# The first weight quarter in two loads of one row each, with three warm-up matmuls fewer

## Chip, cores, metric

The kernel runs on one core of a Trainium2 chip. The metric is device time in microseconds (us). One execution of each kernel was also recorded by the profiler; "the trace" means that one execution. Since it is one of several, its own time is given where that matters.

## The reference, cut

```python
x = A_x                                          # 2048 x 1024, bf16
g = _sigmoid((x * gate_w).sum(-1, keepdims=True))
a = _A_ref(x, A_wqkv, A_wo)                      # linear attention, 32 heads of 32
b = _B_ref(x, B_wqkv, B_wo)                      # sliding dilated attention
return g * a + (1 - g) * b
# in _A_ref:
qkv = x @ wqkv                                   # wqkv: 1024 x 3072, so q | k | v
pq, pk = phi(q), phi(k)
```

The change touches only the very beginning: the k part of A's projection, the first thing that the kernel computes.

## The kernel before: the parts concerned

The weights of k are held in two halves of 512 columns, `WkA[0]` and `WkA[1]`, each with eight "rows" of 128 contraction indices. A "quarter" here is two rows of one half (256 KB). The names used below: the *first* quarter is `WkA[0]` rows 0 and 1, the *second* quarter is `WkA[1]` rows 0 and 1. Two x loads bring 256 of the 1024 columns of token rows 0 to 255 and 256 to 511. TensorE transposes these itself; the rest of x comes transposed by DMA.

```python
def load_wk(eng, k, h):
    eng.dma_start(out=WkA[h][:, 2 * k:2 * k + 2, :],
                  in_=A_wqkv[2 * k * P:(2 * k + 2) * P, D + 512 * h:D + 512 * h + 512]
                  .rearrange("(kt p) n -> p kt n", p=P))
# ... cut
load_wk(nc.scalar, 0, 0)                 # first quarter, on ScalarE's queue
load_rows(nc.sync, 0, 2, 0, 2 * P)       # x rows, on SyncE's queue from here on
load_rows(nc.sync, 2, 4, 0, 2 * P)
load_wk(nc.sync, 0, 1)                   # second quarter
load_xT(1, 0, 4)                         # x transposed by DMA
load_wk(nc.sync, 1, 0)
load_wk(nc.sync, 1, 1)
# ... cut
warm_up(29)                              # 29 matmuls on ones, results unused
# ... cut
transpose_rows(0)
first = [bank_k(i) for i in range(4)]
for kt in range(2):
    for t in range(2):
        project(first[t], t, kt, 0)      # first four real matmuls: first quarter
transpose_rows(2)
first += [bank_k(i) for i in range(4, 8)]
for half, t0 in ((1, 0), (0, 2), (1, 2)):
    for kt in range(2):
        for t in (t0, t0 + 1):
            project(first[4 * half + t], t, kt, half)   # fifth matmul on: second quarter
```

TensorE executes in this order. The last part of the diff concerns `WoB[1]`, weights for the last stage, loaded some 350 us later.

The softmax here doesn't subtract the row's maximum and nothing guards it: scores larger than these inputs give would overflow.

Of the kernel before, what the change touches and what calls it, by code (L numbers as in the profile page):

```python
# [15 lines left out]
P = 128  # L16
# [23 lines left out]
def kernel(  # L40
# [11 lines left out]
    nc = tc.nc  # L52
    S, D = A_x.shape[1:]
# [5 lines left out]
    def rows(ap, s0, s1):  # L59
        return ap[s0 // 1024, s0 % 1024:(s1 - 1) % 1024 + 1, :]  # L60
# [3 lines left out]
    KT = D // P  # L64
# [11 lines left out]
    def load_w(name, src, col0, tag, only=(0, 1)):  # L76
        halves = []
        for h in only:
            w = wpool.tile([P, KT, 512], BF16, name=f"{name}{h}", tag=tag)
            c0 = col0 + h * 512  # L80
            nc.sync.dma_start(out=w[:], in_=src[:, c0:c0 + 512].rearrange("(kt p) n -> p kt n", p=P))
            halves.append(w)
        return halves
# [4 lines left out]
    def load_rows(eng, t0, t1, d0=0, d1=D):  # L88
        eng.dma_start(out=xrow[:, t0:t1, d0:d1],
                      in_=rows(x, t0 * P, t1 * P)[:, d0:d1].rearrange("(t p) d -> p t d", p=P))  # L90

    WkA = [wpool.tile([P, KT, 512], BF16, name=f"WkA{h}", tag="wa") for h in range(2)]

    def load_xT(k, t0, t1):
        nc.sync.dma_start_transpose(out=xT[:, 2 * k:2 * k + 2, t0 * P:t1 * P],
                                    in_=rows(x, t0 * P, t1 * P)[:, 2 * k * P:(2 * k + 2) * P])
# [5 lines that stand above are left out]
# [11 lines left out]
            nc.vector.tensor_tensor(out=ident[q:q + 32, q:q + 32], in0=col[q:q + 32, :], in1=row[q:q + 32, :],  # L113
                                    op=ALU.is_equal)
    with tc.manual_schedule(engines={SP, mybir.EngineType.Activation}):
        load_wk(nc.scalar, 0, 0)
        load_rows(nc.sync, 0, 2, 0, 2 * P)
        load_rows(nc.sync, 2, 4, 0, 2 * P)
        load_wk(nc.sync, 0, 1)
        load_xT(1, 0, 4)  # L120
        load_wk(nc.sync, 1, 0)
        load_wk(nc.sync, 1, 1)
        for k in range(2, 4):
            load_xT(k, 0, 4)
            load_wk(nc.sync, k, 0)
            load_wk(nc.sync, k, 1)
        for t in range(4, NB):
            nc.sync.dma_start_transpose(out=xT[:, :, t * P:(t + 1) * P], in_=rows(x, t * P, (t + 1) * P))
        load_rows(nc.sync, 0, 4, 2 * P, D)
        for t in range(4, NB, 4):  # L130
            load_rows(nc.sync, t, t + 4)
        gw_row = consts.tile([P, D], BF16, name="gw_row")
        nc.sync.dma_start(out=gw_row[:], in_=gate_w.partition_broadcast(P))
        WvA = load_w("WvA", A_wqkv, 2 * D, "wb")
        WoA = load_w("WoA", A_wo, 0, "wo")
        WvB = load_w("WvB", B_wqkv, 2 * D, "wc")
# [49 lines left out]
    with tc.manual_schedule(engines={PE}):  # L186

        with ExitStack() as s1:
# [9 lines left out]
            def warm_up(n):  # L198
                warm = ps_1.tile([P, P], F32, name="warm", tag="p1")
                for i in range(n):  # L200
                    nc.tensor.matmul(warm[:], lhsT=ones, rhs=ones, start=True, stop=True)  # L201


            warm_up(29)
            def transpose_rows(t):
                for kt in range(2):
                    xt = ps_1.tile([P, 2 * P], BF16, name="xt_ps", tag="p1")
                    for i in range(2):
                        nc.tensor.transpose(xt[:, i * P:(i + 1) * P], xrow[:, t + i, kt * P:(kt + 1) * P], ident)  # L209
                    (nc.scalar.copy if kt else nc.vector.tensor_copy)(out=xT[:, kt, t * P:(t + 2) * P], in_=xt[:])  # L210
# [35 lines left out]
            for t in range(1, NB):  # L246
                side.append(lambda t=t: nc.vector.tensor_tensor(
                    out=zacc[:], in0=zacc[:] if t > 1 else pk[:, 0, :], in1=pk[:, t, :], op=ALU.add))
            side.append(lambda: nc.gpsimd.partition_all_reduce(zrow[:], zacc[:], P, bass_isa.ReduceOp.add))
            for t in range(NB):  # L250
                side.append(lambda t=t: nc.vector.tensor_tensor_reduce(
                    out=gjunk[:], in0=xrow[:, t, :], in1=gw_row[:], scale=1.0, scalar=0.0, op0=ALU.mult,
# [139 lines left out]
        with ExitStack() as s2:  # L392
# [157 lines left out]
            WoB = [wpool.tile([P, KT, 512], BF16, name="WoB0", tag="wb")]  # L550

            def load_wo(half, k0, k1):
                for k in range(k0, k1):
                    nc.sync.dma_start(out=WoB[half][:, k, :],
                                      in_=B_wo[k * P:(k + 1) * P, half * 512:(half + 1) * 512])

            for c in range(KT):
                kts[c] = kpool.tile([P, 2, 1024], BF16, name="kt", tag="kt")
                for hh in range(2):
# [3 lines left out]
                    if 1 <= c <= 2:  # L563
                        t = 2 * (c - 1) + hh
                        nc.sync.dma_start_transpose(out=pqT[0][:, :, t * P:(t + 1) * P],
                                                    in_=pqd[t * P:(t + 1) * P, :])
                    if 4 <= c < 7:
# [1 line left out]

            load_wo(0, 6, 8)  # L570
            WoB.append(wpool.tile([P, KT, 512], BF16, name="WoB1", tag="wb"))
            load_wo(1, 0, 4)
            nc.sync.dma_start(out=WoB[1][:, 4:KT, :],
                              in_=B_wo[4 * P:, 512:1024].rearrange("(k p) n -> p k n", p=P))
            raw = wpool.tile([P, 4, D], BF16, name="raw", tag="wc")
            fw = wpool.tile([P, 2, D], F32, name="fw", tag="wc")
            lw = wpool.tile([P, 4, D], BF16, name="lw", tag="wa")
# [112 lines left out]
```

## Time and profile before

| | before |
|---|---|
| median of 3 runs (range) | 472.19 us (471.96 to 472.64) |
| time of the traced run, and its span | 471.98 us, 470.3 us |
| TensorE busy | 466.4 us, 99% |
| first real matmul | 4.75 us |
| fifth, the first to use the second quarter | 5.96 us |
| second quarter landed (semaphore record) | 5.91 us |

"idle before <-releaser" at the end of a timeline line says how long the engine stood and what ended it. Two lines of the timeline of the kernel before belong beside those that the prediction shows, the second transposes and what follows them:

```profile
5.63 0.39 PE L209 MATMUL xt_ps<-pk,xrow 128*128 128x128 bf16 x4
...
5.96 3.41 PE L195 MATMUL pk_ps<-WkA,xT 128*128 128x512 bf16 x15
```

The second line shows no wait, and yet there was one. The instruction records behind these lines have the four transposes start at 5.63, 5.69, 5.74 and 5.80 us, 0.056 us apart, while each is booked 0.22 us long. The last is thus booked until 6.02, and an idle time in front of the fifth matmul can't show, although TensorE was free for it at 5.80 + 0.056 = 5.85 (worked out).

What it waited for is in the trace's semaphore records, which no view prints as such: each load updates its semaphore 16 times, and with the 16th it has *landed*. The second quarter landed at 5.91, and the fifth matmul started 0.05 us later. So TensorE waited about 0.1 us for that load in the kernel before already, and this will matter.

### The profile page before, as it was taken

How to read it: one execution, taken by the hardware profiler on the slowest of the kernel's cores; microseconds unless marked ns; L12 is line 12 of the kernel's file. 1: busy time of each engine (PE TensorE's matmuls, PEld its weight loads, DVE VectorE, ACT ScalarE, POOL GpSimd, SP SyncE). 2: the span in 40 equal slices, each digit the busy share in tenths (PEclk: the TensorE clock that was granted, in tenths of full speed). 3: DMA queues.
4: the chain of work that ended last, by engine and by line, in shares of the span. 5: the costliest groups of instructions: out<-in, count | busy, mean ns of one | idle time of the engine just before them, and what ended most of it. 6: DMA issues, size and time to landing. Idle time of an engine off the chain costs nothing.

```text
span 470.3 us, 13208 instructions
## 1 busy us (share of the span) xinstructions
PE 466.4 (99%) x5765; PEld 266.0 (57%) x5765; DVE 278.1 (59%) x612; ACT 169.6 (36%) x277; POOL 15.3 (3%) x30
## 2 busy tenths in 40 slices
PE   9999999999999999999999999999999999999997
PEld 5444444445444444444888888888764444444444
DVE  2586689990219999999666676667660049800000
ACT  1443321112433333334555555555543134221121
POOL 3300000500000000000000000000000000000000
PEclk9999999999999999999999999999999999999999
DMA  8999960000654243627326525452454933211111
GB/s 242 192 257 366 348 205 0 0 1 1 216 134 123 83 141 123 156 97 252 105 56 106 109 47 97 103 92 55 87 137 102 199 94 79 73 52 45 34 33 46
DMA packets 98188, 55.14 MB, mean 117 GB/s; under 512 B 69074, under 2 KB 90578, under 8 KB 98130
## 3 DMA queue, kind: packets, MB, share of 16 engines
q1 hardware_dynamic: 93106, 49.87, 40.6%
q10 hardware_dynamic: 5024, 4.43, 2.9%
q8 instruction: 45, 0.74, 0.7%
q14 instruction: 13, 0.11, 0.1%
HBM read 26.10 MB, written 15.86 MB: 89 GB/s over the span
## 4 chain that ended last, share of the span: by engine, by line
PE 99%; DVE 0%; issue 0%; DVEq 0%
PE q_ps L419 26%; PE d_ps L625 12%; PE pk_ps L195 12%; PE p_ps L323 12%; PE g_ps L262 12%; PE e_ps L625 12%; PE p_ps L359 9%; PE po L499 2%; PE s2b L477 2%; PE warm L201 1%; PE kv_ps L282 0%; PE w_ps L179 0%; PE xt_ps L209 0%; DVE osb L632 0%; DVE xT L210 0%
## 5 line engine op out<-in xcount | busy, mean ns | idle before, releaser
L419 PE MATMUL q_ps<-xT,WqB 64*64 64x512 bf16 x1024 | 70.1, 376 | 0.0
L419 PE MATMUL q_ps<-xT,WkB 64*64 64x512 bf16 x1024 | 69.7, 376 | 0.0
L170 DVE TENSOR_SCALAR e<-e 128x512 f32<-128x512 f32 x64 | 27.0, 423 | 61.3 <-ACT e L169 61.3
L323 PE MATMUL p_ps<-WvB,xT 128*128 128x512 bf16 x256 | 57.4, 379 | 0.0
L195 PE MATMUL pk_ps<-WkA,xT 128*128 128x512 bf16 x256 | 55.6, 379 | 0.3 <-DVE xT L210 0.3
L262 PE MATMUL g_ps<-pk,xrow 128*128 128x512 bf16 x256 | 55.4, 379 | 0.0
L482 ACT ACTIVATE PT<-s2b 128x928 bf16<-128x928 f32 (+4 forms) x40 | 34.2, 855 | 50.1 <-PE s2b L477 49.1
L484 DVE TENSOR_TENSOR PT<-PT,mask 128x928 bf16<-128x928 bf16 (+4 forms) x40 | 23.6, 589 | 36.3 <-ACT PT L482 36.3
L419 PEld LDWEIGHTS <-WkB 64*64 64x64 bf16 x1024 | 39.7, 107 | 7.3 <-DMA vd<-tmp 0.2
L359 PE MATMUL p_ps<-WqA,xT 128*128 128x512 bf16 x192 | 43.4, 379 | 0.0
L625 PEld LDWEIGHTS <-pqT 128*128 128x128 bf16 x272 | 26.0, 98 | 29.6 <-DMA obd<-Ob 0.2
L625 PEld LDWEIGHTS <-OBT 128*128 128x128 bf16 x272 | 26.0, 98 | 29.4
L262 PEld LDWEIGHTS <-xrow 128*128 128x128 bf16 x256 | 25.0, 98 | 30.2
L419 PEld LDWEIGHTS <-WqB 64*64 64x64 bf16 x1024 | 38.6, 107 | 6.1 <-DVE qz L459 0.2
L195 PEld LDWEIGHTS <-xT 128*128 128x128 bf16 x256 | 24.9, 98 | 30.3 <-DVE xT L210 0.4
L323 PEld LDWEIGHTS <-xT 128*128 128x128 bf16 x256 | 24.9, 98 | 30.2 <-issue 0.5
L632 DVE TENSOR_SCALAR osb<-e_ps,omg 128x128 bf16<-128x128 f32 x1 | 0.3, 350 | 57.6 <-PE e_ps L625 57.6
L328 ACT CAST tmp<-p_ps 128x512 bf16<-128x512 f32 x32 | 18.7, 587 | 38.0 <-PE p_ps L323 33.7
L499 PEld LDWEIGHTS <-PT 64*56 64x56 bf16 (+2 forms) x1152 | 28.9, 104 | 5.5
L169 ACT ACTIVATE e<-pk_ps 128x512 f32<-128x512 f32 x32 | 18.9, 597 | 35.8 <-PE pk_ps L195 31.6
L359 PEld LDWEIGHTS <-xT 128*128 128x128 bf16 x192 | 18.8, 98 | 22.7
L625 PE MATMUL d_ps<-WoA,pqT 128*128 128x512 bf16 (+1 forms) x136 | 30.9, 370 | 0.0
(71 smaller groups left out, 542.1 us busy)
## 6 DMA issues: line engine op xcount, KB each, us to landing
vd<-tmp SPq DMA_DIRECT2D x16, 264.0 KB
out_dram<-osb ACTq DMA_DIRECT2D x31, 128.0 KB
xrow<-in_A_x_dram SPq DMA_DIRECT2D x3, 1024.0 KB
pqd<-tmp SPq DMA_DIRECT2D x12, 256.0 KB
WvA<-in_A_wqkv_dram SPq DMA_DIRECT2D x2, 1024.0 KB
WoA<-in_A_wo_dram SPq DMA_DIRECT2D x2, 1024.0 KB
WvB<-in_B_wqkv_dram SPq DMA_DIRECT2D x2, 1024.0 KB
WqA<-in_A_wqkv_dram SPq DMA_DIRECT2D x2, 1024.0 KB
```

Of the source, the lines that this page charges most:

```text
L169: nc.scalar.activation(out=e[:], in_=pj[:], func=ACT.Exp)
L170: nc.vector.tensor_scalar(out=e[:], in0=e[:], scalar1=1.0, scalar2=1e-6, op0=ALU.min, op1=ALU.add)
L195: nc.tensor.matmul(pj[:], lhsT=xT[:, kt, t * P:(t + 1) * P], rhs=WkA[half][:, kt, :], start=(kt == 0), stop=(kt == KT - 1))
L262: nc.tensor.matmul(pj[:], lhsT=xrow[:, t, kt * P:(kt + 1) * P], rhs=pk[:, t, half * 512:(half + 1) * 512], start=(t == 0), stop=(t == NB - 1))
L323: nc.tensor.matmul(st["pj"][:], lhsT=xT[:, kt, t * P:(t + 1) * P], rhs=WvB[half][:, kt, :], start=(kt == 0), stop=(kt == KT - 1))
L328: nc.scalar.copy(out=v[:, half * 16:(half + 1) * 16, 0:Dh], in_=st["pj"][:].rearrange("p (h e) -> p h e", h=16))
L359: nc.tensor.matmul(st["pj"][:], lhsT=xT[:, kt, t * P:(t + 1) * P], rhs=WqA[half][:, kt, :], start=(kt == 0), stop=(kt == KT - 1))
L419: nc.tensor.matmul(banks[o][64 * j:64 * j + 64, :], lhsT=lhsT(r, kt, j), rhs=rhs(r, kt), start=first and kt == 0, stop=kt == KT - 1, skip_ ...
L482: nc.scalar.activation(out=pt[:, :, 0:W_], in_=s2b[:].rearrange("p a b s -> p (a b) s")[:, :, 0:W_], func=ACT.Exp, scale=SCALE)
L484: nc.vector.tensor_tensor(out=pt[:, :, 0:W_], in0=pt[:, :, 0:W_], in1=mask[:, None, base:base + W_].broadcast_to([P, 4, W_]), op=ALU.mult)
L499: nc.tensor.matmul(o2[64 * h:64 * h + w, par, s_, i, :], lhsT=pt[r, i, o:o + w], rhs=V[r, m, 4 * c + i, :], start=True, stop=True)
L625: nc.tensor.matmul(st["ps"][:, 0:n], lhsT=lhsT, rhs=W[c0 // 512][:, c, c0 % 512:c0 % 512 + n], start=(side == 0 and c == 0), stop=(side == ...
```

## The change

The intent: the x rows, which TensorE waits for first, should not stand behind a whole weight quarter. The quarter is cut in two loads. Three warm-up matmuls are taken out so that TensorE is free when the rows come. The number of loads in all is kept by merging one at the end.

```diff
-        load_wk(nc.scalar, 0, 0)
+        for kt in range(2):
+            nc.scalar.dma_start(out=WkA[0][:, kt, :], in_=A_wqkv[kt * P:(kt + 1) * P, D:D + 512])
...
-            warm_up(29)
+            warm_up(26)
...
-            load_wo(1, 0, 4)
-            nc.sync.dma_start(out=WoB[1][:, 4:KT, :],
-                              in_=B_wo[4 * P:, 512:1024].rearrange("(k p) n -> p k n", p=P))
+            load_wo(1, 0, 3)
+            nc.sync.dma_start(out=WoB[1][:, 3:KT, :],
+                              in_=B_wo[3 * P:, 512:1024].rearrange("(k p) n -> p k n", p=P))
```

## The prediction

> **What bounds the kernel now.** I read the page's busy shares and its chain first, then the waits of TensorE, then the first ten microseconds instruction by instruction, because the change lies almost wholly there.
>
> The page of the kernel before, parts 1 and 4:
>
> ```profile
> span 470.3 us, 13208 instructions
> PE 466.4 (99%) x5765; PEld 266.0 (57%) x5765; DVE 278.1 (59%) x612; ACT 169.6 (36%) x277; POOL 15.3 (3%) x30
> ...
> PE 99%; DVE 0%; issue 0%; DVEq 0%
> ```
>
> TensorE is busy 466.4 of 470.3 us and is 99% of the chain that ended last. So only two things move the time: work taken off TensorE, or idle time ahead of it. Idle time in total is 470.3 - 466.4 = 3.9 us. That is also, within rounding, the most that any change of waits alone can give: 0.8%.
>
> The waits of TensorE's matmuls, then those of its weight loads:
>
> ```profile
> PE warm L201 <- PEq L674: 0.8, 1, 0.8
> PE pk_ps L195 <- DVE xT L210: 0.3, 1, 0.3
> ```
>
> ```profile
> PEld L195 <- DVE xT L210: 0.4, 1, 0.4
> ...
> PEld L209 <- DMA xrow<-in_A_x_dram: 0.2, 1, 0.2
> ```
>
> The columns are total us, number of waits, the longest. The reader is to see two places at the start: the first transposes wait 0.2 us for a transfer of x rows (their weight loads do), and the first real matmul waits 0.3 us for the copy of what was transposed.
>
> The timeline of the start (start, duration, engine, line, operation, count, idle before):
>
> ```profile
> 0.80 0.97 SPq L89 DMA_DIRECT2D xrow<-in_A_x_dram  x2
> 0.81 3.01 PEld L201 LDWEIGHTS <-const-bfloat16-1.0 128*128 128x128 bf16 x29 [0.81 <-issue]
> 0.82 0.47 ACTq L99 DMA_DIRECT2D WkA<-in_A_wqkv_dram  x1
> 0.84 3.25 PE L201 MATMUL warm<-const-bfloat16-1.0 128*128 128x128 bf16 x29 [0.84 <-PEq L674]
> ...
> 3.98 0.33 PEld L209 LDWEIGHTS <-xrow 128*128 128x128 bf16 x4 [0.16 <-DMA xrow<-in_A_x_dram]
> 3.98 0.50 PE L209 MATMUL xt_ps<-pk,xrow 128*128 128x128 bf16 x4
> 4.41 0.29 DVE L210 COPY xT<-xt_ps 128x256 bf16<-128x256 bf16 x1 [0.96 <-PE xt_ps L209]
> 4.52 0.37 ACT L210 COPY xT<-xt_ps 128x256 bf16<-128x256 bf16 x1 [2.44 <-PE xt_ps L209]
> 4.75 0.55 PEld L195 LDWEIGHTS <-xT 128*128 128x128 bf16 x4 [0.44 <-DVE xT L210]
> 4.75 1.04 PE L195 MATMUL pk_ps<-WkA,xT 128*128 128x512 bf16 x4 [0.27 <-DVE xT L210]
> ```
>
> The real work starts at 4.75 us and is unbroken from there. The start time of that matmul is what the change can move. It hangs on transposes (3.98), these on the later of two things: the end of 29 warm-up matmuls in TensorE's order, and the landing of the x rows. The warm-up weight loads end at 0.81 + 3.01 = 3.82, and then the next one sits 0.16 us until the transfer. So the rows land at about 3.9 to 3.98, almost exactly when the warm-up is over. **The warm-up is just long enough to fill the wait; the transfer is the bound, by about 0.1 us.**
>
> The data movement in the same stretch (window, length, busy engines, granted clock, DMA share, GB/s):
>
> ```profile
> 2.00:2.50 0.50, 0.50 (x8) 0.50 (x6) 0.42 (x3) 0.08 (x1) 0.00 (x0) 1.00 0.37 93
> 2.50:3.00 0.50, 0.50 (x7) 0.50 (x6) 0.45 (x4) 0.00 (x0) 0.00 (x0) 1.00 0.64 191
> 3.00:3.50 0.50, 0.50 (x8) 0.50 (x6) 0.43 (x3) 0.00 (x0) 0.00 (x0) 1.00 0.99 335
> 3.50:3.75 0.25, 0.25 (x5) 0.25 (x3) 0.00 (x0) 0.00 (x0) 0.00 (x0) 1.00 1.14 373
> ```
>
> By 3.0 us only (93 + 191) x 0.5 = 142 KB have moved; by 3.5 us 310 KB, by 3.75 us 403 KB. The first x rows (128 KB) and the whole first weight quarter (256 KB) are 384 KB together, reached just before 3.75 us. The rows therefore seem to arrive with the whole weight quarter, not ahead of it.
>
> **What the Trainium skill says.** "DMA: Bandwidth & Descriptors", section "Queues, rings and completion order": every engine turns between the queues that have work at the granularity of a packet, typically 9 to 17 descriptors. The same page, section "Issuing engines are not separate DMA queues": loads issued by ScalarE and by SyncE run on the same 16 engines and interleave. The byte count above fits rows and weights sharing the engines, but the order of the packets is not in the trace. "TensorE: Matmul & The Clock Gate", section "Part 1: The HAM clock gate": the array starts at half clock, and is released after a busy window of about 3.4 us that runs freely; cold spacing is 107 ns at 128 columns. The trace agrees: the median warm-up matmul lasts 311 ns, and 12 of them take 1.49 us, so (1.49 - 0.31) / 11 = 107 ns apart; the shortest of the 29 lasts 265 ns, and the median transpose 219. So the release falls near 4 us, about 3.1 us after TensorE began. The granted-clock column says 1.00 throughout and does not show this. The same page, "Part 4: PE-mode transpose", states that transposes do not count as busy for that gate; no view of this kernel tells.
>
> **The change part by part.**
>
> 1. *The weight quarter in two loads.* One load of 256 KB becomes two of 128 KB on ScalarE's queue. Adds one issue: the one shown took 0.47 us, so the second would go out at about 1.29 us and end at 1.76. ScalarE has nothing to do between its table load (to 2.07) and its copy at 4.52; the issue is free. With 128 partitions over 16 engines, a load of 256 rows is 16 pieces of 1 KB per engine, a half 8 pieces of 1 KB, the x rows 16 pieces of 512 B. If an engine serves a load as one packet, the x rows stand behind at most 8 KB of weights in place of 16 KB. That is 128 KB less for all engines; at 335 to 373 GB/s, 0.34 to 0.38 us earlier. The rows then land near 3.6. The second weight half lands when the whole used to, before about 4.0, and is wanted only by the third matmul, two spacings of 0.22 us (1.04 - 0.38, over 3) after the first. It does not bind.
>
> 2. *Three warm-up matmuls fewer.* 3 x 107 ns = 0.32 us less, so the 26th ends its weight load near 3.5 and TensorE is free for the transposes at about 3.65. This gives nothing alone, since the rows land at 3.9; with part 1 it lets the earlier landing through. Part 1 alone would give at most 0.1 us. The two sizes, 0.32 and 0.36 us, match closely, which makes me believe that the split was tuned for it.
>
> 3. *The last weights, WoB1, in 3 + 1 loads in place of 4 + 1.* One issue less on SyncE's queue near 350 us, 0.4 to 0.6 us there; the number of loads in all stays as before. These weights are wanted after 7 x 8 + 4 x 8 + 3 = 91 matmuls of the last stage, 91 x 0.216 = 19.7 us after its start at 356.7, so at 376; issued at 351 and 640 KB large, they have over 20 us. Worth 0.
>
> Sum if all steps hold: the start of the real work goes from 4.75 to about 4.43, -0.32 us. Does it reach the end? From 4.75 to 468 TensorE's matmuls show no other wait, so an earlier start only fails if a later transfer then binds. The next weights and transposed x that matmul 17 wants at about 8.6 us are 1.28 MB in the order of issue; the stretches of the DMA view sum to about 1.3 MB at 7.0 us. Margin 1.6 us, over 0.3. So -0.3 us passes to the end: 472.19 - 0.32 = 471.87, or 0.07%.
>
> **The rivals.**
>
> *A. The rows do not land earlier* (the engines interleave piece by piece, or the rows' queue was first anyway, its issue being 0.02 us ahead). Then TensorE idles about 0.3 us more before the transposes and everything from 3.98 stays: 472.19, change 0. For it: only 52 KB had moved by 2.5 us, so the second half is queued long before the first is through, and piecewise sharing would be as before. Against it: the matching sizes. I give it 30%.
>
> *B. The clock is released later.* 0.3 us of busy time goes out of the first window, and if transposes do not count, more. If the gate then misses one window of 3.4 us, matmuls of 512 columns run at about 427 ns (estimate, 512 / 1.2 by the clock page) in place of 216 from 4.4 to about 7.4: half of 3 us is lost, +1.5 us, net +1.2 with part 1's gain: 473.4, or +0.25%. For it: the release comes near 4 us, with little to spare. Against it: TensorE would still be busy from 0.84 to about 3.8. I give it 12%.
>
> *C. The extra issue or changed order delays a later transfer* and TensorE stalls at its first use, 0 to 0.5 us; 5%. SyncE's order is unchanged, which speaks against it.
>
> **Range and chances.** 53% for -0.32, 30% for 0, 12% for +1.2, 5% for +0.3 make about -0.17 + 0 + 0.14 + 0.02 = 0 in the mean, but the likeliest outcome is lower. I predict 472.0. The three runs before spread from 471.96 to 472.64, 0.7 us, so the spread is as large as the effect. A range of 471.4 to 472.8 holds the first two cases with that spread; case B lies outside. A 2% change would be 9.4 us, while all idle time of TensorE is 3.9: faster by over 2% is next to impossible, and slower needs a break of the schedule that nothing in the diff makes: 0.5% each.
>
> **What would show it.** In the timeline of the changed kernel: 26 warm-ups from about 0.84; transposes near 3.65 if step 1 holds, near 3.98 with a longer wait of the weight loads for the x rows if A holds; the first real matmul near 4.43 against 4.75. If B holds, the first matmuls last about 600 ns and not 379, and stand 427 ns apart. The span should be 470.0. I am wrong if the first matmul has moved by 0.3 us and the end has not, or if the time is beyond 1 us of the time before.

## The result, and the profile after

The changed kernel took 472.53 us (median of 6, 472.16 to 472.85), the kernel before 472.12 us (median of 6, 471.94 to 472.69). The ratio is 1.0006, with a 95% interval of 0.9993 to 1.0019. Ratios are the mean time of one kernel's runs over that of the other's of the same rounds, so not quite the ratio of the medians. By the interval the two are the same; where a difference of a third of a microsecond comes from must be read in the trace. The traced run of the changed kernel is the slowest of its six (472.85), that of before (471.98) among the fastest, so the two traces lie farther apart than the medians.

Page of the changed kernel, parts 1 and 4:

```profile
span 471.1 us, 13202 instructions
...
PE 98%; DMA 1%; SPq 0%; issue 0%; DVE 0%; DVEq 0%
```

In the chain that ended last, a DMA has appeared with 1%. The waits of TensorE's matmuls (total us, times, longest) say which:

```profile
PE pk_ps L196 <- DMA WkA<-in_A_wqkv_dram: 0.5, 1, 0.5
PE q_ps L420 <- issue: 0.3, 1, 0.3
PE pk_ps L196 <- DVE xT L211: 0.2, 1, 0.2
```

The first two are new. The timeline of the start (line numbers are one higher than before):

```profile
0.83 0.90 ACTq L117 DMA_DIRECT2D WkA<-in_A_wqkv_dram  x2
0.84 2.93 PE L202 MATMUL warm<-const-bfloat16-1.0 128*128 128x128 bf16 x26 [0.84 <-PEq L675]
...
3.71 0.35 PEld L210 LDWEIGHTS <-xrow 128*128 128x128 bf16 x4 [0.21 <-DMA xrow<-in_A_x_dram]
...
4.49 1.17 PE L196 MATMUL pk_ps<-WkA,xT 128*128 128x512 bf16 x4 [0.17 <-DVE xT L211]
...
5.50 0.39 PE L210 MATMUL xt_ps<-pk,xrow 128*128 128x128 bf16 x4
...
6.34 2.98 PE L196 MATMUL pk_ps<-WkA,xT 128*128 128x512 bf16 x13 [0.45 <-DMA WkA<-in_A_wqkv_dram]
```

Read against before: the transposes start at 3.71 and not 3.98, the first matmul at 4.49 and not 4.75. The intent has worked. Then the first four matmuls take 1.17 and not 1.04 us, so the second transposes are only 0.13 us ahead (5.50 against 5.63). And the fifth matmul, which wants the second quarter, stands 0.45 us and starts at 6.34 in place of 5.96. The lead of 0.26 us has become a lag of 0.38.

The chain in order of time, changed kernel:

```profile
1.83 4.46 DMA WkA<-in_A_wqkv_dram
6.29 0.05 issue
6.34 2.76 PE pk_ps L196 x12
```

The chain no longer runs over the warm-up and the rows at all. It goes through one load, the second quarter, issued at 1.83 us as before (1.81), and landed only at 6.29 (5.91 before).

From there on the two kernels are alike. The next stage starts at 60.52 before and at 60.90 after, 54.56 us after the fifth matmul in both. The one other difference is a stop in the traced run of the changed kernel near 351 us:

```profile
351.57 0.41 PE L420 MATMUL q_ps<-WqA,xT 64*64 64x512 bf16 x4 [0.33 <-issue]
```

From the start of the second stage to the last VectorE copy before the final store it is 467.57 - 60.52 = 407.05 us before and 468.44 - 60.90 = 407.54 us after. So the two differ by 0.38 at the start and 0.49 around 351 us, 0.87 together. Is either of them the change, or chance?

Where was the second quarter held up? The DMA view by queue (packets, MB, share of the 16 engines; q1 is SyncE's queue, q10 ScalarE's). First the kernel before, from 2.0 to 3.0 us and from 4.0 to 4.5 us:

```profile
q1 hardware_dynamic: 188, 0.10, 37.2%
q10 hardware_dynamic: 45, 0.05, 13.3%
...
q1 hardware_dynamic: 236, 0.19, 112.8%
```

The changed kernel, the same stretches:

```profile
q10 hardware_dynamic: 150, 0.14, 47.8%
q1 hardware_dynamic: 220, 0.11, 36.2%
...
q1 hardware_dynamic: 112, 0.11, 90.2%
```

With the smaller first load, ScalarE's queue starts sooner (150 packets by 3 us against 45). But from 4.0 to 4.5 us, when the second quarter is on its way, SyncE's queue moves 112 packets in place of 236, while the engines count as 90% busy: the same packets take longer each.

### The profile page after: what moved, and what is told of

Same layout as the page of the kernel before. It is cut to its first block, busy times and chain, and to the rows that moved or that the text cites. A ratio compares the mean times of both kernels' runs of the same rounds, so it can differ in the third digit from the quotient of the medians.

```text
span 471.1 us, 13202 instructions
## 1 busy us (share of the span) xinstructions
PE 466.6 (99%) x5762; PEld 269.3 (57%) x5762; DVE 278.1 (59%) x612; ACT 169.7 (36%) x277; POOL 15.3 (3%) x30
## 4 chain that ended last, share of the span: by engine, by line
PE 98%; DMA 1%; SPq 0%; issue 0%; DVE 0%; DVEq 0%
PE q_ps L420 26%; PE d_ps L626 12%; PE p_ps L324 12%; PE g_ps L263 12%; PE pk_ps L196 12%; PE e_ps L626 12%; PE p_ps L360 9%; PE po L500 2%; PE s2b L478 2%; DMA WkA<-in_A_wqkv_dram 1%; PE kv_ps L283 0%; PE w_ps L180 0%; SPq L89 0%; DVE osb L633 0%; DVEq L633 0%
## 5 line engine op out<-in xcount | busy, mean ns | idle before, releaser
L500 PEld LDWEIGHTS <-PT 64*56 64x56 bf16 (+2 forms) x1152 | 29.9, 104 | 4.4
```

The source lines that it names most:

```text
L500: nc.tensor.matmul(o2[64 * h:64 * h + w, par, s_, i, :], lhsT=pt[r, i, o:o + w], rhs=V[r, m, 4 * c + i, :], start=True, stop=True)
```

## The experiments

All of them were timed in five rounds against the kernel before. Two tables give what the traces show. The first has when the transposes of the first x rows start, the length of the first four matmuls, the end of the last packet of the second quarter, the longest packet of a weight load among those that started before that end, and the start of the fifth matmul. The two packet columns are counted from the trace's packet records, the others are timeline lines. A packet record doesn't name its load; in e9, e10 and e11, where a plain load follows, the end of the second quarter's packets is approximate, and in e6 that of its first half can't be told.

```
kernel                   first      four      second quarter  longest   fifth    median us
                         transp.    matmuls   ends            packet    matmul   (ratio to before, 95%)
no split
 before                  3.98       1.04      5.02            < 0.2     5.96     472.19
 e3 merge only           3.96       1.29      4.98            < 0.2     6.27     472.16 (0.9997; 0.9984 to 1.0010)
 e4 26 warm-ups only     4.05       1.04      5.07            0.29      6.11     472.50 (1.0008; 0.9994 to 1.0022)
 e11 other load order    3.88       1.89      5.15            0.41      6.67     472.87 (1.0013; 1.0000 to 1.0025)
split
 changed kernel          3.71       1.17      5.89            0.84      6.34     472.53 (1.0006; 0.9993 to 1.0019)
 e1 the same again       3.78       1.56      5.88            1.13      6.33     472.70 (1.0006; 0.9993 to 1.0019)
 e2 split only           3.88       1.05      6.00            1.14      6.45     472.59 (1.0007; 0.9994 to 1.0019)
 e5 second on ScalarE q. 3.66       1.05      7.39            2.17      7.79     473.00 (1.0022; 1.0006 to 1.0039)
 e6 second split too     3.75       1.59      ? and 6.24      0.86      6.27     472.35 (0.9999; 0.9986 to 1.0012)
 e7 matmul order         3.67       1.73      6.35            1.83      6.68 *   472.43 (1.0006; 0.9995 to 1.0018)
 e8 half on SyncE's q.   3.71       see text  6.31            1.74      7.25     474.45 (1.0047; 1.0035 to 1.0059)
 e9 two loads between    3.75       1.63      5.76            1.06      6.34     472.38 (1.0006; 0.9993 to 1.0018)
 e10 one load between    3.69       1.89      5.77            0.95      6.66     472.64 (1.0010; 0.9996 to 1.0024)
 e12 third row ScalarE   3.72       1.04      6.30            0.58      6.78     472.84 (1.0008; 0.9994 to 1.0021)
* in e7 the fifth matmul uses the first quarter
```

The second table is from the clock and semaphore records of the same traces and the instruction records behind the timeline: when TensorE was granted the full rate, when the second quarter landed, when TensorE was free for the fifth matmul (start of the last transpose and one spacing, worked out), and when it started.

```
kernel                   full rate   second quarter   TensorE free   fifth
                         from        landed           for fifth      matmul
no split
 before                  4.23        5.91             5.85           5.96
 e3 merge only           no record   6.22             6.09           6.27
 e4 26 warm-ups only     4.55        6.06             5.93           6.11
 e11 other load order    6.52        5.50             6.67           6.67
split
 changed kernel          4.80        6.29             5.72           6.34
 e1 the same again       5.67        6.29             6.18           6.33
 e2 split only           4.76        6.41             5.80           6.45
 e5 second on ScalarE q. 4.50 **     7.74             5.55           7.79
 e6 second split too     5.68        6.22 and 6.60    6.18           6.27
 e7 matmul order         no record   6.75             another order
 e8 half on SyncE's q.   9.98        6.73             7.25           7.25
 e9 two loads between    5.76        6.30             6.22           6.34
 e10 one load between    6.68        6.62             6.58           6.66
 e12 third row ScalarE   4.12        6.73             5.60           6.78
** and half rate again from 7.92 to 11.33
```

Three things can be read from it.

- In all eleven traces in which the second quarter landed after TensorE was free, the fifth matmul started 0.04 or 0.05 us after the landing, in the kernel before too. What comes earlier in TensorE's order didn't set that time.
- With the load order of the kernel before, the second quarter landed at 5.91 to 6.22 in the three traces without the split and at 6.29 to 6.75 in the four with it (the changed kernel, e1, e2, e7). That is 0.37 us later in the mean, but the nearest two are 0.07 apart: that it is later with the split has held in every trace, while its size varies by about as much as the effect.
- The last packet is not the landing. From the one to the other it took 0.9 to 1.2 us in those three traces without the split and 0.4 us in those four with it. So the end of the packets moved by 0.87 us in the first pair of traces and the landing by 0.38.

### e1: the changed kernel again

No edit. 

> The changed kernel again, unedited, for a second trace. In the first trace three things moved: the first real matmul came 0.26 us earlier (4.49 against 4.75 us), TensorE then waited 0.45 us for the weight load of SyncE's queue until 6.34 us, and at 351 us it stood 0.33 us in a wait with no cause shown. Theory T1 (the late weight load belongs to the split): the wait until about 6.3 us comes again, within 0.1 us. Rival R1 (it is chance of the single run): the matmul starts at about 5.9 us with no wait on that load. For the stop near 351 us: if it belongs to the change it comes again, if not it is missing. Time: 472.2 to 472.9.

Measured 472.70 (472.30 to 473.14); traced run 472.32. Its timeline:

```profile
4.56 1.56 PE L196 MATMUL pk_ps<-WkA,xT 128*128 128x512 bf16 x4 [0.17 <-DVE xT L211]
...
5.39 0.15 PEld L196 LDWEIGHTS <-xT 128*128 128x128 bf16 x1 [0.28 <-issue]
...
6.33 0.98 PEld L196 LDWEIGHTS <-xT 128*128 128x128 bf16 x6 [0.16 <-DMA WkA<-in_A_wqkv_dram]
```

The fifth matmul starts at 6.33, as in the first trace (6.34), although this time the first four took 1.56 us and the transposes were later. The second quarter landed at 6.29 in both. The wait shows only at a weight load (0.16), because the matmuls' booked lengths cover it; TensorE was free at 6.18. Expectation T1 held, R1 fell. The stop near 351 us is not there (407.01 us from the second stage to the end, as before): it was chance.

The 1.56 us is the second finding. Weight loads alone with 0.28 us of unexplained "issue" ahead of them, one every 0.43 us, are what a TensorE at half rate looks like: at full rate these matmuls stand 0.22 apart. So in this trace the full rate came late; the clock record has it granted from 5.67 us, when three of the first four matmuls had started.

### e2: only the split

```diff
 # kernel before, with only:
-        load_wk(nc.scalar, 0, 0)
+        for kt in range(2):
+            nc.scalar.dma_start(out=WkA[0][:, kt, :], in_=A_wqkv[kt * P:(kt + 1) * P, D:D + 512])
```

> Only the split of the first weight quarter; 29 warm-ups and the last weights as before. T1: the x rows land at about 3.7 us as in the changed kernel, but the transposes start no earlier than the end of the warm-up, about 3.93 us (3.98 before); the first real matmul at 4.70; and the weight load of SyncE's queue is late, with a wait until about 6.3 us. R1: no wait at 6 us. Time: T1 472.5, R1 472.1.

Measured 472.59; the timeline:

```profile
4.69 1.05 PE L196 MATMUL pk_ps<-WkA,xT 128*128 128x512 bf16 x4 [0.17 <-DVE xT L211]
...
6.45 0.82 PE L196 MATMUL pk_ps<-WkA,xT 128*128 128x512 bf16 x3 [0.49 <-DMA WkA<-in_A_wqkv_dram]
```

Close to what T1 said: first matmul at 4.69 (4.70 was expected; the 29 warm-ups now bind, and the transposes' weight loads start at 3.78 without a wait), and a wait of 0.49 us for the second quarter until 6.45. So the load is late with the split alone (it landed at 6.41); the shorter warm-up is not needed for it.

### e3: only the merge of the last weights

```diff
-            load_wo(1, 0, 4)
+            load_wo(1, 0, 3)
 # and the load behind it from row 3 in place of 4
```

> Only the last weights in 3 + 1 loads. Theory T2 (the stop of 0.33 us near 351 us belongs to the larger merged load, which holds the DMA engines): the stop is there. Rival R2 (it belongs to the shift of the loads in between, or to chance): no stop; the trace is that of before all through, first matmul at 4.75 us, and the time 472.1.

Measured 472.16, ratio 0.9997. No stop near 351 us (407.02 us to the end). T2 fell: the merged load costs nothing. The start should have been that of before, and the rows came so (3.96), but the first four matmuls took 1.29 us: a late full rate is thus not tied to the change. It cost nothing here, for TensorE was free at 6.09 and the second quarter landed only at 6.22. That is 0.31 us later than in the trace of before, and 0.07 earlier than in the changed kernel, although nothing at the start was edited: part of the lag of the first pair of traces can be chance.

### e4: only three warm-ups fewer

```diff
-            warm_up(29)
+            warm_up(26)
```

> Only three warm-ups fewer, the first weight quarter in one load. The prediction said this gives nothing alone: TensorE idles about 0.3 us more before the transposes, which stay at 3.9 to 3.98 us, and the first real matmul stays at 4.70 to 4.75 us. Rival (the clock gate is released later when the warm-up is shorter): first matmuls longer than 379 ns and over 0.3 us apart, time 473 or more. Time otherwise 472.1.

Measured 472.50 (472.01 to 473.86). The timeline:

```profile
4.05 0.61 PE L209 MATMUL xt_ps<-pk,xrow 128*128 128x128 bf16 x4 [0.28 <-DMA xrow<-in_A_x_dram]
```

TensorE stands 0.28 us for the rows, which come no earlier (4.05), and the first matmul follows at 4.83 against the 4.70 to 4.75 expected. The four matmuls took 1.04 us: no late full rate in this trace, so the rival fell here. The cut of the warm-up gains nothing alone, as expected.

### e5: the second quarter on ScalarE's queue

```diff
 # changed kernel, with:
+        load_wk(nc.scalar, 0, 1)          # behind the two halves
-        load_wk(nc.sync, 0, 1)
```

> The changed kernel, with the second weight quarter (the load that TensorE waited for at 6.3 us) moved from SyncE's queue to the end of ScalarE's. In the three traces with the split that load's packets began at 3.5 to 3.7 us and ended at 5.9 to 6.0, with a few packets of 0.6 to 1.1 us near 4 us; in the three without it they began at 3.7 to 3.9 and ended at 5.0 to 5.1. Theory T3 (the split lets ScalarE's queue run dry at 3.6 to 4.1 us, after which this load has to share SyncE's queue with the transposing loads behind it): on ScalarE's queue it lands by about 5.2, the wait is gone, the second group of matmuls starts with the end of the transposes at about 5.7 us, and the next stage starts at 60.3 in place of 60.9; time 471.9. Rival R3 (packets near 4 us stall whatever they carry): the wait is as long, or moves to another load; the stage starts at 60.9, time 472.6.

A clear miss for T3, and a cost: 473.00 us, ratio 1.0022. The traced run, at 475.47 the slowest of six (the others 472.31 to 473.25), exaggerates it:

```profile
7.79 2.23 PE L196 MATMUL pk_ps<-WkA,xT 128*128 128x512 bf16 x5 [2.08 <-DMA WkA<-in_A_wqkv_dram]
...
8.53 0.15 PEld L196 LDWEIGHTS <-xT 128*128 128x128 bf16 x1 [0.28 <-issue]
```

The load landed at 7.74 us. Its packets took 0.3 to 0.6 us each near 4 us and up to 2.17 us near 5, side by side with the first packets of the transposing load on the other queue. And after 2.08 us of standing, TensorE ran at half rate (the single weight loads with 0.28 us of issue; the clock record says from 7.92 to 11.33 us), though its first four matmuls had been at full rate (1.05 us). In this run the wait cost more than its length.

### e6: the second quarter in two loads as well

```diff
-        load_wk(nc.sync, 0, 1)
+        for kt in range(2):
+            nc.sync.dma_start(out=WkA[1][:, kt, :], in_=A_wqkv[kt * P:(kt + 1) * P, D + 512:D + 1024])
```

> The changed kernel, with the second weight quarter too in two loads of one row each, on SyncE's queue. T3: the packets of the first half still meet the transposing loads late; the first half lands earlier than the whole, at about 5.2, so the first two matmuls of the group start at 5.7 and the wait, of about 0.2 us, is in front of the third; the next stage starts at about 60.6. R3 (stalls near 4 us hit the first half, which is in flight then): the first half lands at 5.5 or later and the wait is hardly shorter, stage start 60.8 to 60.9. Time 472.2 against 472.6.

Measured 472.35, ratio 0.9999. The last packet of the two halves ended at 6.24 us, with packets of up to 0.86 us; the first half landed at 6.22 and the second at 6.60. The fifth matmul started at 6.27, 0.05 us after the first landing. So R3's "5.5 or later" came and T3's 5.2 did not, although the wait is hardly seen, since the first four matmuls took 1.59 us. The time equals that of before and is not below it.

### e7: another order of the first matmuls

```diff
-            for half, t0 in ((1, 0), (0, 2), (1, 2)):
+            for half, t0 in ((0, 2), (1, 0), (1, 2)):
```

> The changed kernel, with the loads untouched but the order of the first matmuls changed: the first weight half for token rows 2 and 3 before the second weight half for rows 0 and 1. The late load is then wanted 4 x 0.22 = 0.86 us later. If the wait for it is what costs 0.38 us, it disappears; in its place comes the wait for the copies of the second transposes (to 6.10 and 6.29 us in the first trace of the changed kernel), so the group starts at about 6.15 in place of 6.34 and the next stage at about 60.7. Rival (the load is even later than the wait shows, or the next ones are late too): a wait of similar length farther on, stage start 60.9. Time 472.3 against 472.6.

Measured 472.43. No wait for the second quarter is left in the trace, though it landed only at 6.75 (it is now wanted at 7.55); a wait of 0.28 us for VectorE's copy has taken its place, as expected. But the first four matmuls took 1.73 us, 0.69 more than at full rate, so the stage started at 61.24 and not at 60.7. The wait can be moved out of the way; whether time is won by it does not show beside this.

### e8: the second row of the split on SyncE's queue

```diff
         nc.scalar.dma_start(out=WkA[0][:, 0, :], in_=A_wqkv[0:P, D:D + 512])
 # and on SyncE's queue, ahead of the second quarter:
+        nc.sync.dma_start(out=WkA[0][:, 1, :], in_=A_wqkv[P:2 * P, D:D + 512])
```

> The changed kernel, with only the first row of the split on ScalarE's queue and the second on SyncE's, behind the x rows. It asks which part of the split brings the x rows forward and delays the second weight quarter. If it is the smaller first load alone, the rows land as in the changed kernel (transposes at 3.7 to 3.8 us). The second row then lands near 4.5, in time for the third matmul at 4.9; the second weight quarter is 128 KB further back on its queue, so it lands at 6.3 or later (T3 and R3 both), and the stage starts at 60.9 to 61.2. If the rows are back at 3.95, the order of arrival on ScalarE's queue is the cause instead. Time 472.6 to 472.9.

The transposes start as in the changed kernel (3.71), so the smaller first load alone brings them forward. The rest went beyond the expectation: 474.45 us in the median, 474.24 to 474.63 in all five runs, ratio 1.0047. The timeline, then the stretch from 7.0 to 9.5 us (length, busy engines, granted clock, DMA share, GB/s):

```profile
6.01 1.01 PE L196 MATMUL pk_ps<-WkA,xT 128*128 128x512 bf16 x2 [0.49 <-DMA WkA<-in_A_wqkv_dram]
...
8.10 0.15 PEld L196 LDWEIGHTS <-xT 128*128 128x128 bf16 x1 [0.28 <-issue]
```

```profile
7.00:9.50 2.50, 2.50 (x11) 1.10 (x9) 0.29 (x1) 0.37 (x1) 0.00 (x0) 1.00 1.11 283
```

The last packet of the first quarter's second row ended at 5.47 us and the row landed at 5.97 (expected 4.5), so the third matmul waited until 6.01. In this trace the full rate was granted only from 9.98 us: the matmuls up to there stand 0.43 us apart. The next stage starts at 63.15, 2.25 us after that of the changed kernel. This is the prediction's rival B in full size. It comes here with a wait in the middle of the first matmuls and not with a shorter warm-up, which is that of the changed kernel. The last fence is a warning: TensorE counts as 100% busy and the granted clock as 1.00 in a stretch at half rate. The clock record of a trace begins with its first change, 9.98 us here, and the view takes the time before it as 1.00. The number of matmuls (11 in 2.5 us) betrays the half rate.

### e9, e10, e11: what stands behind the second quarter

```diff
 # e9: changed kernel with          e11: kernel before with the same
-        load_xT(1, 0, 4)
         load_wk(nc.sync, 1, 0)
         load_wk(nc.sync, 1, 1)
+        load_xT(1, 0, 4)
 # e10: changed kernel, load_xT between the two load_wk
```

> The changed kernel, with the first transposing load of SyncE's queue moved behind the next two plain weight loads. Counted in the packets of the trace, the second weight quarter's last packet ended at 5.9 to 6.4 us in all traces with the split and SyncE's old order, and at 5.0 to 5.1 in all without the split; some of its packets took 0.4 to 1.8 us from 3.5 to 4.3 us on. Theory T4 (the split lets some engines run ahead into the transposing load behind it, and that holds the rest up): with plain loads behind it, the second quarter ends by about 5.0 and no packet of it takes over 0.4 us; TensorE does not wait at 6 us, the group starts at about 5.7, or when the clock is released late at up to 6.3 as the transposes come later; next stage at 60.3 to 60.8, time 471.9 to 472.2. Rival R3 (packets stall near 4 us whatever is behind them): last packet at 5.8 or later, stage start 60.9, time 472.6.

> The same with one plain weight load between in place of two. T4: 256 KB of plain load, 0.7 us at some 350 GB/s, stand between the second quarter and the transposing load, so the second quarter still ends by about 5.1; the held-up packets are those of the load in between, which is wanted only at about 8.3 us. Stage start 60.3 to 60.8, time 471.9 to 472.2. R3: as in the changed kernel, 60.9 and 472.6.

> The kernel before (no split, 29 warm-ups, last weights in 4 + 1), with only the order of the loads of the last but one run (transposing load behind two plain weight loads). There the second quarter was in time already: both theories expect no gain from it, stage start 60.5 to 60.8, time 472.2, within 0.3 of before. If it is faster than before by 0.3 us or more, the order helps by itself, and a gain of the run with the split can't be put down to the split.

Theory T4 blamed the transposing load right behind the second quarter. With plain loads in its place the second quarter's packets still ended at about 5.76 (e9) and 5.77 us (e10), with packets of 1.06 and 0.95 us that began near 4.1, and it landed at 6.30 and 6.62. As the cause of the slow packets, T4 fell.

The landings say something else, though. Without the split (e11) the second quarter landed at 5.50, 0.4 to 0.7 us earlier than in the three traces with the transposing load behind it. And in all three runs of this edit it is now the load directly ahead of the transposing one that is held up: some of its 16 updates come early, then there is a pause of 0.86 to 1.85 us, and the rest come about 0.01 us apart. In before, e3 and e4 the second quarter has that pause, of 0.34 to 0.69 us; in the changed kernel, e1, e2 and e7 it is 1.0 to 1.5. So a transposing load goes with a late landing of the load ahead of it, with the split and without; why, no view tells.

The other order brings no time in any of the three (472.38, 472.64, 472.87 us). e11 has one of the two longest half-rate starts (1.89 us, with 29 warm-ups), and its transposing load now binds in its turn: the chain that ended last runs over that load, landed at 9.43, to a matmul at 9.48.

### e12: a third row on ScalarE's queue

```diff
-        for kt in range(2):
+        for kt in range(3):                # on ScalarE's queue
 # and SyncE's load of that quarter reduced to its other row
```

> The changed kernel, with a third row of weights (128 KB of the quarter that is wanted at about 8.3 us) behind the two on ScalarE's queue, taken off SyncE's. It keeps ScalarE's queue at work until after 4 us, while the second weight quarter runs on SyncE's. T3 (that load is slow because ScalarE's queue has run dry): the second quarter's last packet ends by about 5.4 us (5.05 without the split, and 128 KB at some 350 GB/s is 0.37 us), no packet of it takes over 0.4 us, TensorE does not wait for it at 6 us, next stage at 60.3 to 60.8, time 471.9 to 472.2. R3 (packets near 4 us stall in any case once the split is there): last packet at 5.8 us or later, the wait near 6.3 us comes again, stage start 60.9 or later, time 472.6 to 472.9.

Measured 472.84, ratio 1.0008. In the trace TensorE is at full rate from its first matmul (4.50 us, four in 1.04), and then waits:

```profile
6.78 5.57 PE L196 MATMUL pk_ps<-WkA,xT 128*128 128x512 bf16 x25 [1.02 <-DMA WkA<-in_A_wqkv_dram]
```

The last packet came at 6.30, and the load landed at 6.73. ScalarE's queue was at work until 5.9, so an idle queue is not the cause: T3 fell for good. Packets on both queues took 0.3 to 0.6 us from 3.7 us on.

## Why the prediction was right or wrong

**The frame held, the mechanism did not.** 472.0 was predicted with 471.4 to 472.8, and 472.53 was measured. That it lies in the range is owed to the width of the range, which was made to hold the case of no gain too; the predicted step was 0.3 us faster, and the medians went 0.4 us the other way. The prediction named its own sign of being wrong, "if the first matmul has moved by 0.3 us and the end has not": it moved by 0.26 us, and the end did not follow. That nothing here can reach 2% followed from 3.9 us of idle time, and held for every run, the worst median of which is 0.5% away.

**Part 1, the rows come earlier: right, a little oversized.** Predicted 0.34 to 0.38 us; the transposes went from 3.98 to 3.71, 0.27 us, and they start at 3.66 to 3.78 us in every trace with both the split and the shorter warm-up. Rival A (30%) is thus refuted. That the smaller first load does it is shown by e8; whether by the order of packets that the prediction assumed is not. The second row of the first quarter bound nothing, as said.

**Part 2, the warm-ups: right.** Alone they give nothing (e4: 4.83); the split alone gives 0.06 us at the first matmul (e2: 4.69 against 4.75, at most 0.1 was predicted); together 0.26.

**Part 3, the last weights: right.** Worth 0 (e3).

**The step that failed is "Does it reach the end?".** The prediction read that "from 4.75 to 468 TensorE's matmuls show no other wait", said that an earlier start "only fails if a later transfer then binds", and looked at the weights "that matmul 17 wants at about 8.6 us". A later transfer did bind, and had bound before the change: the second quarter, wanted by the fifth matmul. In the kernel before it landed at 5.91, TensorE was free at 5.85, and the matmul started at 5.96. The prediction took "no wait shown" for "room", and there was none. So an earlier first matmul could not reach the end, even if this load had landed as before. In the changed kernel it landed at 6.29, and 0.38 us came out as lag. (For matmul 17 the margin was about 0.8 us and not 1.6: its weights landed at 7.79, where the prediction went by the bytes moved by 7.0.)

**This is rival C in kind**, "the extra issue or changed order delays a later transfer", which had 5% and 0 to 0.5 us. The argument against it, that SyncE's order is unchanged, was weak: the prediction itself had written that loads of both queues interleave on the same engines.

**Rival B, the clock: not as put, but present.** The length of the start at half rate varies from run to run, with the old warm-up as with the new: the first four matmuls take 1.04, 1.05, 1.29 and 1.89 us in the traces with 29 warm-ups and 1.04 to 1.89 us in those with 26 where nothing else interrupts them. So no effect of the three warm-ups can be seen. In the changed kernel much of a late clock hides behind the wait for the second quarter (e1: 1.56 us, and still 6.33).

**What the times say.** Over the first comparison and the one of e1, the changed kernel has a mean of 472.61 us in 11 runs, the kernel before 472.31 in 15. The 0.30 us agree with the 0.38 us of the traces, but both intervals contain 1. That the second quarter's landing sets the fifth matmul is shown by eleven traces; that it lands later with the split, by seven with small distances; a slowdown in time is likely and not shown.

**What stays open** is why packets of 1 KB that are on their way from about 3.5 to 4.4 us take 0.4 to 1.8 us in the split kernels and not in the others (in e11 the first of 0.41 us starts at 4.66, and longer ones follow in the next load), and why the load ahead of a transposing load lands so late. The first is not the warm-up (e2), not the transposing load behind (e9, e10), not an idle queue of ScalarE (e12), and not the queue that the load is on (e5). Slow packets as such are not the split's: those of the transposing load take up to 0.44 us in before (from 5.08) and 0.78 in e3 (from 5.33). No version was found that beats both kernels; e6 equals the kernel before.

## What to carry to other kernels

Before counting an earlier start as a gain, list what each of the next few instructions needs and when that lands; a wait that does not show has an unknown margin, not a large one, and where matmuls are booked longer than their spacing (0.22 against 0.056 us here) there can be a wait that the views don't show. Cutting one load brought its neighbour forward by 0.27 us here and went with a landing of another 0.38 us later, so read the landing of every load in flight, not only of the one moved, and take the last semaphore update for it, not the last packet. For effects below a microsecond, trace the same kernel at least twice: one of two losses in the first trace here was chance.

## What the Trainium skill lacked or had wrong

- "TensorE: Matmul & The Clock Gate", "Part 1: The HAM clock gate": it gives an idle window of about 3.4 us before the array goes back to half rate. In e5 a wait of 2.08 us between matmuls was enough: the clock record has full rate from 4.50 to 7.91 us and half rate from 7.92 to 11.33. Each stretch lasts 3.41 us, which agrees with the window's length, but in the first TensorE still worked for over a third of the time. That the windows run freely, so the release varies, agrees too: full rate is granted from 4.12 to 6.68 us in ten of the eleven other traces with a record, and from 9.98 in e8.
- The same section warns not to trust single clock records. In these traces they agree with the spacing of matmuls wherever there is one, but two of 14 traces (e3, e7) have none, and none tells of the time before the first change: the 1.00 of e8 from 7.0 to 9.5 us, with 11 matmuls in 2.5 us, stands there.
- "DMA: Bandwidth & Descriptors", "Issuing engines are not separate DMA queues": it says that loads of all issuing engines interleave on the same DMA engines and that spreading them saves only issue time. It has no figure for what that means for one load. Here a smaller load on one queue went with other landings on the other queue: the first x rows at 3.67 and not 3.94 us, the second quarter at 6.29 and not 5.91.
- No page tells of single 1 KB packets that take 0.4 to 1.8 us beside others of the same load whose median is about 0.05 us; the runs show them from about 3.5 us on in all ten traces with the split (up to 2.17 us in e5).
- No page says that a load directly ahead of a transposing load on the same queue lands late. The second quarter landed at 5.91 to 6.22 us with such a load behind it and at 5.50 without (e11), and in e9, e10 and e11 the pause in the completion moved to the load that then stood there.
